# An attention and feed-forward kernel: the first batch's start rearranged, and the halves of the attention weights made on ScalarE and GpSimd

## The chip, the cores and the metric

The kernel runs on one core of one Trainium2 chip. The metric is the device time of one launch in microseconds (us). Each kernel was run several times, and medians and ranges are given.

## The reference

```python
B, N, m, C = 4, 12416, 32, 128                 # x: (B, N, C); inducing: (m, C)

def mab(q, kv):
    s = scale * (q @ kv.transpose(0, 2, 1));  s = s - s.max(-1, keepdims=True)
    a = np.exp(s);  a /= a.sum(-1, keepdims=True) + 1e-09
    return a @ kv

h = mab(I, x)                                  # 32 inducing points look at all tokens
x = mab(x, h).reshape(B * N, C)                # each token looks at the 32 points

rms = np.sqrt(np.mean(x * x, axis=-1, keepdims=True) + 1e-06)
xn = x / rms * rms_g
g = xn @ w_gate                                # 128 -> 1536
silu = g * (1.0 / (1.0 + np.exp(-g)))
return (silu * (xn @ w_val)) @ w_out           # 1536 -> 128
```

The weights arrive as 64-bit numbers and are rounded to 32 bits on the chip.

## The kernel before

The kernel has two parts in time. The **start-up** (to about 61 us) loads x of the first batch, makes its scores and h, and rounds the first weights. The **feed-forward part** follows: some 1,200 steps, each with two products with the gate and value weights (`L600`, `L605`), a silu on ScalarE, a multiplication on VectorE (`u`) and a product with `w_out` (`L550`). The later batches' attention work is threaded through these steps. The parts that matter here:

```python
def warm(n):                                   # products without use, to hold TensorE's clock
    ps = ps_acc.tile([P, 512], F32, name="acc")
    for _ in range(n):
        nc.tensor.matmul(ps[:, 0:P], ident[:], ident[:], start=True, stop=True)
...
def parts():                                   # rounding, step 1 (VectorE): exponent e and fraction f
    ...
    nc.vector.tensor_scalar(out=e[:], in0=high, scalar1=20, scalar2=0x7FF, ...)
    nc.vector.tensor_scalar(out=e[:], in0=e[:], scalar1=896.0, scalar2=1151.0, op0=ALU.max, op1=ALU.min)
    nc.vector.tensor_scalar(out=f[:], in0=high, scalar1=0xFFFFF, scalar2=None, op0=ALU.bitwise_and)
def place(engine): ...                         # step 2 (ScalarE or GpSimd): as floating point
def join(): ...                                # step 3 (VectorE twice, then a product on GpSimd)
```

At a **seam** (one of 27 places, after the first tile, where the next tile of tokens is prepared) the attention weights are turned and cut into a rounded part and a rest, both for TensorE:

```python
def split():
    aT = work.tile([P, 512], F32, name="aT", tag="work")
    nc.vector.transpose(out=aT[rows, 0:w], in_=sc[b][rows, cols2[s]])
    hi, lo = split_of[b, s] = [halves.tile([P, 512], F32R, name=k) for k in ("hi", "lo")]
    nc.vector.tensor_copy(out=hi[rows, 0:w], in_=aT[rows, 0:w])
    nc.vector.tensor_tensor(out=lo[rows, 0:w], in0=aT[rows, 0:w], in1=hi[rows, 0:w].bitcast(F32), op=ALU.subtract)
```

In part of the steps the product with `w_out` is made as three quick ones (a **split product**) instead of one slow one. Its operands cost two operations on ScalarE and two subtractions on GpSimd, some 2.6 us of GpSimd:

```python
nc.scalar.activation(hi, v, AF.Copy, scale=1.0 - 2.0 ** -13)          # v is u
nc.gpsimd.tensor_tensor(out=lo, in0=v, in1=hi.bitcast(F32), op=ALU.subtract)
def rest():
    hs = third.tile([P, 512], F32, name="hs")
    nc.scalar.activation(hs[:, 0:T], hi.bitcast(F32), AF.Copy, scale=2.0 ** -12)
    nc.gpsimd.tensor_tensor(out=d, in0=hs[:, 0:T], in1=lo.bitcast(F32), op=ALU.subtract)
```

A planner decides at build time which steps are split. It keeps an account of when GpSimd is free; `seam_busy` is time of GpSimd that it leaves for a seam's steps (step 5 is `split`):

```python
seam_busy[at] = seam_busy.get(at, 0) + {2: 1.4, 3: 3.0, 4: 1.2}.get(i, 0)
...
free = max(free, now) + busy.get(k, 0) + seam_busy.get((b, u, j), 0)
begin = max(free, now + 2.2 * SLOT)
if (... begin > now + 3.2 * SLOT ...):
    continue                                   # no split product in this step
free = begin + SPLIT
```

## Time and profile before

| | |
|---|---|
| time, first three runs | 1717.77 us median (1717.04 to 1718.19) |
| profiled span, granted clock | 1715.7 us, 0.996 |
| TensorE busy | 1675.3 us (98%) |
| first feed-forward product | at 60.72 us |
| last part | a row of 1,200 steps; a quiet one takes 1.33 us, with a split product 1.17 us |

TensorE is nearly always busy, so the end is set by it alone; what can be won is the time in which it waits or does work of no use. The table of waits of TensorE from 140 to 1690 us names the first kind (what waits, `<-` what released it: us in all, times, longest):

```profile
PE gv L600 <- ACT silu L602: 6.0, 9, 1.0
PE gv L600 <- DVE u L607: 5.9, 9, 0.7
PE acc L550 <- DVE u L607: 4.2, 9, 1.0
```

The second and third lines: some 10 us of waiting for `u`, in pieces of up to 1 us. `u` is made by VectorE, which is only 69% busy, so something stands in front of it now and then.

### The profile page before, as it was taken

The page shows a single profiled execution, that of the slowest core. Times are in us where ns is not written, and L with a number is a line of the kernel's source. Part 1 is how long each engine was busy: PE and PEld are TensorE (multiplying, and loading weights), DVE is VectorE, ACT ScalarE, POOL GpSimd, SP SyncE. Part 2 cuts the span into 40 slices and gives each one's busy share as a digit, 9 for nine tenths or more (in the row PEclk, how much of TensorE's full clock was granted, in tenths as well). Part 3 has the DMA queues.
Part 4 walks back from the last instruction along what each step waited for, and adds up shares of the span by engine and source line. Part 5 has one row for each costly group of instructions (what it writes and reads, how often), then busy time and mean ns, then how long its engine had stood idle before and what let it go on. Part 6 is the DMA issues. An engine that isn't in the chain of part 4 may idle for free. (4 is left out here: it accounts for less than half of the span.)

```text
span 1715.7 us, 23430 instructions
## 1 busy us (share of the span) xinstructions
PE 1675.3 (98%) x6855; PEld 1046.2 (61%) x6855; DVE 1189.4 (69%) x1982; ACT 1222.4 (71%) x2180; POOL 1181.4 (69%) x936
## 2 busy tenths in 40 slices
PE   9899999999999999999999999999999999999998
PEld 7545565655566656665556656566556666666666
DVE  4867876777668776667667877667767666666665
ACT  4346777676777777776777777767677887788786
POOL 0317775776487776676657877577657888888875
PEclk9999999999999999999999999999999999999999
DMA  6344433433343232434334314153211121112111
GB/s 248 87 68 74 81 69 78 103 80 64 62 79 63 47 71 41 105 76 91 67 59 83 58 34 83 36 129 77 50 30 35 32 38 31 35 34 37 31 36 24
DMA packets 389359, 112.65 MB, mean 66 GB/s; under 512 B 365136, under 2 KB 369776, under 8 KB 386672
## 3 DMA queue, kind: packets, MB, share of 16 engines
q1 hardware_dynamic: 388944, 111.02, 32.3%
q8 instruction: 54, 0.88, 0.2%
q14 instruction: 73, 0.60, 0.1%
q10 hardware_dynamic: 288, 0.15, 0.0%
HBM read 53.95 MB, written 27.00 MB: 47 GB/s over the span
## 5 line engine op out<-in xcount | busy, mean ns | idle before, releaser
L607 DVE TENSOR_TENSOR u<-silu,gv 128x512 f32<-128x512 f32 (+2 forms) x1200 | 788.2, 665 | 471.9 <-PE gv L605 276.6
L602 ACT ACTIVATE silu<-gv 128x512 f32<-128x512 f32 (+2 forms) x1200 | 698.6, 584 | 414.7 <-PE gv L600 377.2
L550 PE MATMUL acc<-u,wo 128*128 128x512 f32 (+2 forms) x1598 | 793.9, 581 | 7.0 <-DVE u L607 5.8
L605 PE MATMUL gv<-a,sv 128*128 128x512 f32 (+2 forms) x1200 | 768.1, 640 | 1.3 <-ACT silu L602 0.7
L588 POOL TENSOR_TENSOR xn<-u,xn 128x512 fp32r<-128x512 f32 (+2 forms) x401 | 507.8, 1266 | 314.7 <-ACT xn L587 250.0
L593 POOL TENSOR_TENSOR xn<-hs,xn 128x512 fp32r<-128x512 f32 (+2 forms) x401 | 507.0, 1264 | 53.4 <-POOL xn L588 16.7
L600 PE MATMUL gv<-a,sg 128*128 128x512 f32 (+2 forms) x1200 | 492.5, 410 | 14.3 <-ACT silu L602 6.5
L600 PEld LDWEIGHTS gv<-a,sg 128*128 128x128 f32 x1200 | 227.6, 190 | 255.3 <-ACT silu L602 117.1
L550 PEld LDWEIGHTS acc<-u,wo 128*128 128x128 f32 x1598 | 299.1, 189 | 87.5 <-issue 17.9
L605 PEld LDWEIGHTS gv<-a,sv 128*128 128x128 f32 x1200 | 227.7, 190 | 196.5 <-issue 142.3
L587 ACT ACTIVATE xn<-u 128x512 fp32r<-128x512 f32 (+2 forms) x401 | 248.1, 619 | 18.8 <-DVE u L607 18.1
L592 ACT ACTIVATE hs<-xn 128x512 f32<-128x512 f32 (+2 forms) x401 | 246.3, 614 | 8.8 <-POOL xn L593 8.2
L550 PE MATMUL acc<-xn,xn 128*128 128x512 f32 (+2 forms) x401 | 159.0, 396 | 6.2 <-POOL xn L593 5.9
L568 PE MATMUL u<-xn,xn 128*128 128x512 f32 (+2 forms) x401 | 155.8, 388 | 0.0
L566 PE MATMUL u<-xn,xn 128*128 128x512 f32 (+2 forms) x401 | 155.4, 388 | 0.0
L492 POOL TENSOR_TENSOR rs<-ms,mhalf 128x16 f32<-128x16 f32 (+2 forms) x28 | 75.5, 2698 | 43.0 <-DVE ms L490 42.9
L550 PEld LDWEIGHTS acc<-xn,xn 128*128 128x128 f32 x401 | 75.3, 188 | 29.9 <-POOL xn L593 14.1
L568 PEld LDWEIGHTS u<-xn,xn 128*128 128x128 f32 x401 | 75.4, 188 | 17.1
L566 PEld LDWEIGHTS u<-xn,xn 128*128 128x128 f32 x401 | 75.3, 188 | 15.6
L559 DVE STREAM_TRANSPOSE o<-o 128x512 f32<-128x512 f32 (+2 forms) x97 | 67.7, 698 | 3.4
L558 DVE TENSOR_TENSOR o<-acc,o 128x512 f32<-128x512 f32 (+2 forms) x97 | 64.9, 669 | 0.0
L571 ACT ACTIVATE o<-u 128x512 f32<-128x512 f32 (+2 forms) x97 | 56.4, 582 | 0.2
(155 smaller groups left out, 746.2 us busy)
## 6 DMA issues: line engine op xcount, KB each, us to landing
out_dram<-o SPq DMA_DIRECT2D x320, 64.0 KB, 2.0
xT<-in_x_dram SPq DMA_DIRECT2D x60, 256.0 KB, 4.6
xn<-in_x_dram SPq DMA_DIRECT2D x60, 256.0 KB, 4.4
a<-hi SPq DMA_DIRECT2D x160, 64.0 KB, 2.0
a<-lo SPq DMA_DIRECT2D x158, 64.0 KB, 2.0
w<-w SPq DMA_DIRECT2D x22, 256.0 KB, 3.2
xn<-in_x_dram SPq DMA_DIRECT2D x5, 1024.0 KB, 10.8
out_dram<-o SPq DMA_DIRECT2D x64, 60.0 KB, 2.0
```

Of the source, the lines that this page charges most:

```text
L492: nc.gpsimd.tensor_tensor(out=rs, in0=ms, in1=mhalf[rows, 0:n], op=ALU.pow)
L550: nc.tensor.matmul(acc[:, 0:T], lhsT, rhs, start=st["left"] == NJ, stop=st["left"] == 1)
L566: nc.tensor.matmul(ups[:, 0:T], w[:, i, :], hi, start=st["k"] == nk, stop=False)
L568: nc.tensor.matmul(ups[:, 0:T], w[:, NK + i, :], lo, start=False, stop=not st["k"])
L587: nc.scalar.activation(hi, v, AF.Copy, scale=1.0 - 2.0 ** -13)
L588: nc.gpsimd.tensor_tensor(out=lo, in0=v, in1=hi.bitcast(F32), op=ALU.subtract)
L592: nc.scalar.activation(hs[:, 0:T], hi.bitcast(F32), AF.Copy, scale=2.0 ** -12)
L593: nc.gpsimd.tensor_tensor(out=d, in0=hs[:, 0:T], in1=lo.bitcast(F32), op=ALU.subtract)
L600: nc.tensor.matmul(g[:, 0:T], sg[:, ts(j, P)], a[:, 0:T], start=True, stop=True)
L602: nc.scalar.activation(sl[:, 0:T], g[:, 0:T], AF.Silu)
L605: nc.tensor.matmul(v[:, 0:T], sv[:, ts(j, P)], a[:, 0:T], start=True, stop=True)
L607: nc.vector.tensor_tensor(out=t[:, 0:T], in0=sl[:, 0:T], in1=v[:, 0:T], op=ALU.mult)
```

## The change

It wants three things: (a) a quicker start, with fewer warm-up products, raw weights read only behind all of x, h.T straight out of the summing product (one transpose and some small steps less), and weights rounded beside TensorE's sums; (b) late weights placed on ScalarE in place of GpSimd, which lets their four clamping steps on VectorE go (three more go for weights that ScalarE placed already, so two of nine stay); (c) at the seams, the halves off VectorE: `hi` on ScalarE, `lo` on GpSimd, with 1.4 us of GpSimd kept free for it in the planner. One more edit rides along: the second subtraction of a split product reads `u` instead of `lo`, with another scale, for the same value.

```diff
-    warm(24)
+    warm(10)
...
         def put():
-            if unread:
+            puts.append((i, c))
+            for _ in range((1, 3, 2, 1, 0, 0, 0, 0, 0)[len(puts) - 1]):
                 fetch_raw(*unread.pop(0))
...
-            nc.vector.tensor_scalar(out=e[:], in0=e[:], scalar1=896.0, scalar2=1151.0, op0=ALU.max, op1=ALU.min)
+            if clamp:
+                nc.vector.tensor_scalar(out=e[:], in0=e[:], scalar1=896.0, scalar2=1151.0, op0=ALU.max, op1=ALU.min)
...
-                    if engine is nc.scalar:
+                    if engine is nc.scalar and t is st["e"]:
+                        nc.scalar.activation(to[:], t[:], AF.Relu, bias=bias[:], scale=mul)
+                    elif engine is nc.scalar:
...
-        def end_h():
-            ... fold product, + 1e-9, reciprocal of 128x1, h = product * rec
         def turn_h():
-            ps = st["ps"] = bank()
-            nc.tensor.transpose(ps[:, 0:P], st["h"][:], ident[:])
+            ps, hl = bank(), st["hl"]
+            f = fold[:].rearrange("p q m -> p (q m)")
+            nc.tensor.matmul(ps[:, P:2 * P], hl[:, C:C + 1].to_broadcast((P, P)), f, start=True, stop=True)
+            nc.tensor.matmul(ps[:, 0:P], hl[:, 0:C], f, start=True, stop=True)
+            rec = once.tile([P, P], F32, name="rec")
+            nc.vector.reciprocal(out=rec[:], in_=ps[:, P:2 * P])
             hT = st["hT"] = once.tile([P, P], F32, name="hT")
-            nc.vector.tensor_copy(out=hT[:], in_=ps[:, 0:P])
+            nc.vector.tensor_tensor(out=hT[:], in0=ps[:, 0:P], in1=rec[:], op=ALU.mult)
...
-            nc.vector.tensor_copy(out=hi[rows, 0:w], in_=aT[rows, 0:w])
-            nc.vector.tensor_tensor(out=lo[rows, 0:w], in0=aT[rows, 0:w], in1=hi[rows, 0:w].bitcast(F32), op=ALU.subtract)
+            if b or s:
+                nc.scalar.copy(out=hi[rows, 0:w], in_=aT[rows, 0:w])
+            else:
+                nc.vector.tensor_copy(out=hi[rows, 0:w], in_=aT[rows, 0:w])
+            engine.tensor_tensor(out=lo[rows, 0:w], in0=aT[rows, 0:w], in1=hi[rows, 0:w].bitcast(F32), op=ALU.subtract)
...
-                nc.scalar.activation(hs[:, 0:T], hi.bitcast(F32), AF.Copy, scale=2.0 ** -12)
-                nc.gpsimd.tensor_tensor(out=d, in0=hs[:, 0:T], in1=lo.bitcast(F32), op=ALU.subtract)
+                nc.scalar.activation(hs[:, 0:T], hi.bitcast(F32), AF.Copy, scale=1.0 + 2.0 ** -12)
+                nc.gpsimd.tensor_tensor(out=d, in0=hs[:, 0:T], in1=v, op=ALU.subtract)
...
-    f["end_h"]()
-    warm(6)
-    f["turn_h"]()
     join(2, 0)
     place(0, 1)
+    f["sum_end"]()
+    warm(4)
+    f["turn_h"]()
+    warm(4)
...
-    warm(22)
+    f["stack_of"](0, 0)
+    warm(8)
...
-                (0, place, 0, 2, nc.gpsimd), ...
-                (1, parts, 1, 2), (2, place, 1, 2, nc.gpsimd), (2, join, 0, 2),
+                ... (1, join, 0, 2),
+                (1, parts, 1, 2), (2, place, 1, 2), (3, join, 1, 2),
...
-                seam_busy[at] = seam_busy.get(at, 0) + {2: 1.4, 3: 3.0, 4: 1.2}.get(i, 0)
+                seam_busy[at] = seam_busy.get(at, 0) + {2: 1.4, 3: 3.0, 4: 1.2, 5: 1.4}.get(i, 0)
```

More of the change, by code (lines that the diff above doesn't have):

```diff
@@ L161 @@
     make_identity(nc, ident[:])
+    bias = const.tile([P, 1], F32, name="bias")
+    nc.vector.memset(bias[:], -896.0 * (1 << 23))
     ones = const.tile([P, 1], F32, name="ones")
@@ L188 @@
     chunks = [(i, c) for c in range(NC) for i in ((0, 1, 2) if not c else (0, 1))] + [(2, c) for c in range(1, NC)]
-    places, raw = [], {}
+    places, raw, puts = [], {}, []
     wide = moe_w_gate.dtype != F32
@@ L216, in put, with parts @@
                 nc.sync.dma_start(out=w32[i][c][:], in_=st["dst"])
-            if unread:
+            puts.append((i, c))
+            for _ in range((1, 3, 2, 1, 0, 0, 0, 0, 0)[len(puts) - 1]):
                 fetch_raw(*unread.pop(0))
-        def parts():
+        def parts(clamp=False):
             if i < 2:
@@ L271, in open_ @@
             st["gmx"] = small.tile([P, NS], F32, name="gmx")
+            gram[b] = small.tile([P, P], F32, name="gram")
+            nc.gpsimd.memset(gram[b][:], 0.0)
         def bank():
@@ L344, in turn_e @@
         def turn_e(s):
-            e = st["e", s] = work.tile([P, per[s] * m], F32, name="e", tag="work")
-            nc.vector.transpose(out=e[:], in_=sc[b][:, cols1[s]])
+            e = st["e", s] = (work.tile([P, per[s] * m], F32, name="e", tag="work") if b else
+                              up.tile([P, 512], F32, name="u"))[:, 0:per[s] * m]
+            nc.vector.transpose(out=e, in_=sc[b][:, cols1[s]])
         def sum_h(s):
@@ L361, in sum_h, with sum_end @@
                 nc.vector.tensor_tensor(out=hl[rows, 0:C], in0=hl[rows, 0:C], in1=ps[rows, 0:C], op=ALU.add)
-            elif end:
+            elif end and b:
                 nc.vector.tensor_copy(out=hl[:, 0:C], in_=ps[:, 0:C])
-        def end_h():
-            ps = bank()
-            nc.tensor.matmul(ps[:, 0:C + 1], fold[:].rearrange("p q m -> p (q m)"), st["hl"][:], start=True, stop=True)
-            rec = small.tile([P, 1], F32, name="rec")
-            nc.vector.tensor_scalar_add(out=rec[:], in0=ps[:, C:C + 1], scalar1=1e-9)
-            nc.vector.reciprocal(out=rec[:], in_=rec[:])
-            h = st["h"] = once.tile([P, C], F32, name="h")
-            nc.vector.tensor_scalar_mul(out=h[:], in0=ps[:, 0:C], scalar1=rec[:])
-        def turn_h():
-            ps = st["ps"] = bank()
-            nc.tensor.transpose(ps[:, 0:P], st["h"][:], ident[:])
+        def sum_end():
+            nc.vector.tensor_copy(out=st["hl"][:, 0:C], in_=st["ps"][:, 0:C])
+        def turn_h():
+            ps, hl = bank(), st["hl"]
[4 more added lines that the diff above has]
+            nc.vector.reciprocal(out=rec[:], in_=ps[:, P:2 * P])
             hT = st["hT"] = once.tile([P, P], F32, name="hT")
-            nc.vector.tensor_copy(out=hT[:], in_=ps[:, 0:P])
+            nc.vector.tensor_tensor(out=hT[:], in0=ps[:, 0:P], in1=rec[:], op=ALU.mult)
             if b:
@@ L383, in scale_h @@
             hg = st["hg"] = once.tile([P, P], F32, name="hg")
-            nc.vector.tensor_scalar_mul(out=hg[:], in0=st["ps"][:, 0:P], scalar1=gam[:])
+            nc.vector.tensor_scalar_mul(out=hg[:], in0=st["hT"][:], scalar1=gam[:])
         def square_h():
@@ L389, in square_h @@
                 scale_h()
-            gram[b] = small.tile([P, P], F32, name="gram")
-            nc.gpsimd.memset(gram[b][:], 0.0)
             stacks[b] = [stk.tile([P, F], F32R, name=n) for n in ("sg", "sv")]
@@ L615, with parts @@
     f = attention(0, B > 1)
-    reads = chunks[:len(places)]
-    unread = chunks[len(places):]
+    unread = list(chunks)
     for s in range(NS):
         load_rows(0, s)
-        if reads and s in (0, 2):
-            fetch_raw(*reads.pop(0))
-    for one in reads:
-        fetch_raw(*one)
+        if s in (0, 2):
+            fetch_raw(*unread.pop(0))
     weight = {one: rounding(*one) for one in chunks}
-    def parts(i, c):
-        weight[i, c][0]()
+    def parts(i, c, clamp=False):
+        weight[i, c][0](clamp)
     def place(i, c, engine=nc.scalar):
@@ L635 @@
     f["open_"]()
-    early = [(step, i) for i in range(2) for step in (parts, join)]
+    early = [lambda i=i, first=first: (parts(i, 0, True), place(i, 0, nc.vector)) if first else join(i, 0)
+             for i in range(2) for first in (True, False)]
     for s in range(NS):
@@ L642 @@
         if s and early:
-            step, i = early.pop(0)
-            step(i, 0)
-            if step == parts:
-                place(i, 0, nc.vector)
+            early.pop(0)()
     f["scores1"](NS - 1)
@@ L662 @@
     parts(0, 1)
-    warm(4)
-    f["end_h"]()
-    warm(6)
-    f["turn_h"]()
     join(2, 0)
     place(0, 1)
+    f["sum_end"]()
+    warm(4)
+    f["turn_h"]()
+    warm(4)
     ps = f["scores"](0, f["st"]["hT"][:, 0:m], R, per2[0])
     f["square_h"]()
-    warm(22)
+    f["stack_of"](0, 0)
+    warm(8)
     f["scores2"](0, ps)
@@ L680 @@
     join(0, 1)
-    for i in range(2):
-        f["stack_of"](i, 0)
+    f["stack_of"](1, 0)
     warm(16)
@@ L685 @@
     scale()
+    for i in range(2):
+        f["stack_low"](i, 0)
     parts(1, 1)
     place(1, 1)
-    for i in range(2):
-        f["stack_low"](i, 0)
     apply()
@@ L697 @@
     parts(0, 2)
+    place(0, 2)
     flowing.append(True)
@@ L715, in schedule @@
             for k, step, *args in (
-                (0, place, 0, 2, nc.gpsimd), (0, f["stack_of"], 1, 1), (0, f["stack_low"], 1, 1),
-                (1, parts, 1, 2), (2, place, 1, 2, nc.gpsimd), (2, join, 0, 2),
-                (3, parts, 2, 1), (4, join, 1, 2), (4, place, 2, 1, nc.gpsimd), (5, f["stack_of"], 0, 2), (5, f["stack_low"], 0, 2),
+                (0, f["stack_of"], 1, 1), (0, f["stack_low"], 1, 1), (1, join, 0, 2),
+                (1, parts, 1, 2), (2, place, 1, 2), (3, join, 1, 2),
+                (3, parts, 2, 1), (4, place, 2, 1), (5, f["stack_of"], 0, 2), (5, f["stack_low"], 0, 2),
                 (6, f["stack_of"], 1, 2), (6, f["stack_low"], 1, 2), (6, join, 2, 1),
-                (7, parts, 2, 2), (8, place, 2, 2, nc.gpsimd), (10, join, 2, 2),
+                (7, parts, 2, 2), (8, place, 2, 2), (10, join, 2, 2),
             ):
@@ L743, in schedule @@
                 add(203 + 7 * s, g["sub_max"], s)
-            for k, name in ((126, "max1"), (128, "max2"), (130, "max3"), (134, "exp1"), (189, "end_h"), (191, "turn_h"),
+            for k, name in ((126, "max1"), (128, "max2"), (130, "max3"), (134, "exp1"), (191, "turn_h"),
                             (193, "square_h")):
```

## The prediction

> **What bounds the kernel now.** I read the page first: busy times, then the chain that ended last.
>
> ```profile
> PE 1675.3 (98%) x6855; PEld 1046.2 (61%) x6855; DVE 1189.4 (69%) x1982; ACT 1222.4 (71%) x2180; POOL 1181.4 (69%) x936
> PE 22%; issue 0%; DVE 0%; ACT 0%; POOL 0%; DVEq 0%; POOLq 0%
> ```
>
> TensorE (PE) is busy 98% and the traced end of the chain is all TensorE. But busy is not useful: warm-up matmuls (L178) and matmuls at a lower clock count too. So I read the start and the seams as timelines, where the diff acts. First, TensorE's timeline of the first 63 us (start, duration, then the wait before it):
>
> ```profile
> 1.36 7.99 PE L178 MATMUL acc<-ident 128*128 128x128 f32 x48 [1.36 <-POOL mhalf L165]
> 9.45 3.71 PE L292 MATMUL gv<-ident,xn 128*128 128x128 f32 x32
> 20.26 1.94 PE L292 MATMUL gv<-ident,xn 128*128 128x128 f32 x16 [0.31 <-DMA xn<-in_x_dram]
> 33.05 6.02 PE L358 MATMUL gv<-xn,e 128*32 128x128 f32 x194
> 43.45 5.16 PE L178 MATMUL acc<-ident 128*128 128x128 f32 x44
> 48.44 1.02 PE L478 MATMUL mm<-eT,gram 128*128 128x512 f32 x2
> 60.72 0.47 PE L600 MATMUL gv<-a,sg 128*128 128x512 f32 x1 [1.53 <-DMA a<-lo]
> ```
>
> The feed-forward part begins at 60.72 us; everything ahead of it is start-up. Two groups of warm-up matmuls stand in the way of real work: the first until 9.35, though the first tile of x landed about 5.0 us after its issue at 0.73 (tile view of x, shortest landing), and the 44 until 48.4, though eT was done at 47.09 (46.38 + 0.71).
>
> Second, the complete timeline where the feed-forward part begins:
>
> ```profile
> 62.17 1.37 DVE L237 TENSOR_SCALAR we<-we 128x512 int32<-128x512 int32 x1
> 63.30 1.12 PE L444 MATMUL mm<-silu,hg 128*128 128x512 f32 x2 [1.88 <-POOL silu L256]
> 71.24 2.08 PE L444 MATMUL mm<-w,hg 128*128 128x512 f32 x2 [2.27 <-POOL w L256]
> 86.79 1.12 PE L550 MATMUL acc<-u,wo 128*128 128x512 f32 x2 [1.01 <-POOL wo L256]
> ```
>
> TensorE waits for weights that VectorE and GpSimd are still rounding. The table by windows gives granted clocks of 0.72 and 0.66 for 65-70 and 70-75 us.
>
> Third, a seam, where the next tile's attention weights are cut in halves:
>
> ```profile
> 197.89 1.67 DVE L503 TENSOR_TENSOR lo<-aT,hi 128x512 fp32r<-128x512 f32 x1
> ...
> 200.21 0.50 PE L600 MATMUL gv<-a,sg 128*128 128x512 f32 x1 [0.71 <-DVE u L607]
> ```
>
> The subtraction (L503) holds VectorE 1.67 us, u comes late, TensorE waits.
>
> **What the Trainium skill says.** (1) "SBUF — State Buffer", Who interferes with whom: VectorE and GpSimd share a port pair as an exclusive lock; a VectorE instruction with two SBUF inputs contends with a GpSimd one that reads SBUF, and so does a one-input VectorE instruction in a 2-port mode. The trace agrees: L503 takes 0.69 us when GpSimd is idle and 1.61 us in the median; L237 takes 0.43, but 1.37 beside a GpSimd product. (2) "TensorE: Matmul & The Clock Gate", What's actually happening: the array is at half clock until about 3.4 us of sustained work and falls back after an idle window. The trace agrees roughly: 7 matmul records per us from 3 to 6 us, 11 to 12 at 7 to 9. (3) "VectorE: DVE Perf Modes", First, the fixed hardware budget: the reciprocal is an iterative divide with a repeat count of 8. The trace has it only on 128x1 (0.16 us). My estimate for the new 128x128 form from that page, if the repeats cost a cycle each: 128 x 8 / 0.96 GHz = 1.07, plus 0.16, so 1.2 us. (4) The clock-gate page, Architectural detail, says that ScalarE and VectorE are strict FIFO: rounding put on ScalarE stands in front of the next silu.
>
> **The change part by part.**
>
> *Loading x.* 14 fewer warm-ups, and three raw weights (0.5 MB each) no longer in the queue just behind x. TensorE can start at about 5.8 instead of 9.45, gaining 3.6 if it alone decided. But DMA is at 300 to 460 GB/s until 28 us: six x tiles and two raw weights are 7.3 MB, at 410 GB/s 17.7 us from 2.8, so the sixth tile lands at 20.5 to 21.5 (the first rounded weight is then written and the third raw one read). In before it landed near 22.9 (issued 5.8, 17.1 to landing) and 4.2 us of work followed its transposes' start at 23.12 (to 27.33). The new end is about 25.4: **-1.9**. A cold clock on the first transposes would cost TensorE 1.6, hidden under this limit.
>
> *Summing h.* The exponentials get more buffers (up to eight instead of three). TensorE's 97 summing products take 5.94 us from 33.05 and are almost continuous: **-0.3**. Two parts and a join (some 2.2 us of VectorE) go into this stretch, where VectorE is free from its last transpose until the sums end (2.7 us).
>
> *h.T by the product.* Before, from the fold's end at 40.38 to hT at 42.15 is 1.77 us through four small VectorE steps, one TensorE transpose and the crossings. After: reciprocal 1.2 (estimate) and a multiplication 0.3 plus crossings, 1.6: **-0.2**. hg no longer follows a join: **-0.2**.
>
> *Warm-ups.* 22 become 8 plus one weight product of 0.86 us, ending some 2.6 us earlier; TensorE is then free when eT comes. Of 1.35 us (48.44 - 47.09) I take **-1.1**; VectorE has a join in between.
>
> *Start of the feed-forward part.* In 60-80 us the matmuls counted (20 of L600/L605, 14 records of L550/L444) are worth 20 x 0.2335 + 14 x 0.4315 = 10.7 us at full clock: 9.3 lost. Four clamps go (0.43 to 1.37 each) and GpSimd's placing, and the join for 71.24 comes three steps earlier. Against it, ScalarE takes 8 placings of 0.62 us in front of silus, each waiting for VectorE, and the first gap (1.88) stays because its chain stays. Following the order of the two compiled programs, VectorE reaches u6 about as late as before; I take **-1.5** of 9.3, a choice.
>
> *Seams.* Step lengths (L600 to L600) exceed the quiet ones, 1.33 us plain and 1.17 with a split product, by 16.6 us summed over the 26 later seams; about 14 of it belongs to the halves (the rest beside an exponential). With hi on ScalarE (0.6) and lo on GpSimd (1.28), VectorE keeps only the 0.7 us transpose: I take **-11.4**, some 80%.
>
> *Fewer split products.* The planner now reserves 1.4 us of GpSimd per seam, and the compiled programs have 383 split products instead of 401: 18 x (1.33 - 1.17) = **+2.9**.
>
> *Later batches.* The long reciprocal sits on VectorE three times: **+0.5**. Changing the subtraction's second operand to u keeps its length: 0.
>
> Sum: -1.9 - 0.3 - 0.4 - 1.1 - 1.5 - 11.4 + 2.9 + 0.5 = -13.2. 1717.8 - 13.2 = 1704.6, so **1705 us**.
>
> **Rivals.** *ScalarE becomes the wait.* The silu wait for TensorE (377 us in all, in short pieces) says that it has room; but one stuck placing or hi copy stops silu. If that gave back the start's gain and half the seams', 1712. *GpSimd becomes the wait.* At 69% and 1.28 us per operation it now gets 27 subtractions; split products already wait for L593 3.2 us after 140 us. If seams gain only 5, 1711. *The start gains fully.* If DMA stops limiting and the weights' gaps vanish with the cold clock, the start gives 12 instead of 5: 1698. *The loading is hidden anyway:* if weights read later arrive late for parts, their wait replaces the first saving: 1707.
>
> **Range and chances.** Start -1 to -11 and steady part -2 to -12, seldom both at an extreme: 1697 to 1712. Two per cent is 34 us, more than all lost time that the diff touches (some 9 in the start's ramp, 14 at seams, 5 ahead). Faster 0.02, within 2% 0.97, slower 0.01.
>
> **What would show it.** First transposes near 5.8 and the sixth x tile near 21; score end near 25.4; first L600-type product near 57; reciprocal near 1.2 us; no 2.27 us wait at the third late weight; no VectorE halves beyond the first; TensorE's waits for u at seams gone; 383 split products. Wrong if silus wait for placings, if late raw weights stall VectorE, or if TensorE waits for GpSimd at seams.

## The result, and the profile after

| | before | after |
|---|---|---|
| median (range) of 4 runs each | 1717.51 us (1717.04 to 1718.19) | 1709.34 us (1707.92 to 1710.3) |
| ratio, 95% interval | 1 | 0.9951 (0.9934 to 0.9969) |
| profiled span | 1715.7 us | 1708.1 us |
| split products | 401 | 383 |

The change gains 8 us, within 2%.

The page of the kernel after, busy times and the chain that ended last:

```profile
PE 1668.0 (98%) x6781; PEld 1036.0 (61%) x6781; DVE 1145.0 (67%) x1914; ACT 1224.3 (72%) x2179; POOL 1146.2 (67%) x919
PE 87%; ACT 4%; DVE 3%; issue 2%; POOL 2%; DMA 1%; SPq 1%; ACTq 0%; DVEq 0%; POOLq 0%
```

VectorE has 44 us less to do, but the end has moved by 8: that is the first sign that its work was mostly not on the path. To see where the 8 us arose I took the start of each feed-forward step (its first product with the gate weights) in both traces and subtracted. The **lag** after minus before, in us:

```
step        0     2     8    14    84    96   300   600   900  1188
lag     -0.96 +0.05 +1.06 +1.33 +1.74 +0.97 +0.25 -1.76 -3.73 -7.60
```

So the start-up gained 1.0 us, the first 14 steps lost 2.3, and from there on 8.9 us were gained. The prediction's total (-13.2) misses by 5; its split (start -3.7, first steps -1.5, the rest -8.0) misses most in the first two.

TensorE's timeline of the start-up, after:

```profile
5.79 1.97 PE L301 MATMUL gv<-ident,xn 128*128 128x128 f32 x16 [0.36 <-DMA xn<-in_x_dram]
10.63 3.18 PE L301 MATMUL gv<-ident,xn 128*128 128x128 f32 x16 [2.88 <-DMA xn<-in_x_dram]
...
26.94 1.12 PE L310 MATMUL gv<-xT,indT 128*32 128x480 f32 x16
...
33.72 5.65 PE L368 MATMUL gv<-xn,u 128*32 128x128 f32 x194
...
47.04 1.12 PE L485 MATMUL mm<-eT,gram 128*128 128x512 f32 x2 [0.63 <-DVE eT L479]
...
59.76 0.47 PE L610 MATMUL gv<-a,sg 128*128 128x512 f32 x1 [2.73 <-DMA a<-lo]
```

TensorE does begin on x at 5.79 instead of 9.45, but then it waits 2.88 us for the second tile, which it begins at 10.63 and transposes in 3.18 us, where a tile takes 1.97 at full clock: the granted clock was 0.66 from 10 to 15 us (1.00 before). The scores end at 28.06 (26.94 + 1.12); before, they ended at 27.39. The first feed-forward product waits 2.73 us for its operand (1.53 before): TensorE is through with its work ahead of that wait 2.2 us earlier (57.02 against 59.18, the ends of the last warm-up products), and 1.2 of it is waited away.

All engines' timeline of the first feed-forward steps, after:

```profile
65.75 0.60 ACT L612 ACTIVATE silu<-gv 128x512 f32<-128x512 f32 x1 [0.20 <-PE gv L610]
...
67.96 1.49 DVE L243 TENSOR_SCALAR o<-sc 128x512 int32<-128x512 int32 x1
...
69.37 0.68 DVE L617 TENSOR_TENSOR u<-silu,gv 128x512 f32<-128x512 f32 x1
69.48 0.63 ACT L252 ACTIVATE o<-o 128x512 f32<-128x512 int32 x1 [0.68 <-DVE o L243]
70.02 1.06 ACT L612 ACTIVATE silu<-gv 128x512 f32<-128x512 f32 x2
70.10 0.79 PE L615 MATMUL gv<-a,sv 128*128 128x512 f32 x1 [2.96 <-DVE u L617]
```

The join for the third late weight came earlier and its wait of 2.27 us is gone. In its place TensorE waits 2.96 us, for the `u` at 69.37. Its silu was done at 66.35 (65.75 + 0.60); what held it were VectorE's own steps in front of it, the join (from 66.42 on) and the next weight's first steps, of which the masking (L243) took 1.49 us next to GpSimd's join product. ScalarE had to wait for the same masking with a placing (L252), and the next silu (70.02) stood behind that. And the clock was granted at 0.50 from 70 to 75 us (0.66 before).

TensorE's waits from 140 to 1690 us, after:

```profile
PE gv L610 <- ACT silu L612: 8.3, 15, 1.0
PE acc L560 <- POOL xn L603: 3.4, 6, 0.7
PE acc L560 <- DVE u L617: 1.5, 6, 0.3
```

The seam's wait for `u` in front of the gate product (5.9 us) is gone, as planned. The wait for silu grew from 6.0 in 9 places to 8.3 in 15.

### The profile page after: what moved, and what is told of

Same layout as the page of the kernel before. It is cut to its first block, busy times and chain, and to the rows that moved or that the text cites. A ratio compares the mean times of both kernels' runs of the same rounds, so it can differ in the third digit from the quotient of the medians.

```text
span 1708.1 us, 23142 instructions
## 1 busy us (share of the span) xinstructions
PE 1668.0 (98%) x6781; PEld 1036.0 (61%) x6781; DVE 1145.0 (67%) x1914; ACT 1224.3 (72%) x2179; POOL 1146.2 (67%) x919
## 4 chain that ended last, share of the span: by engine, by line
PE 87%; ACT 4%; DVE 3%; issue 2%; POOL 2%; DMA 1%; SPq 1%; ACTq 0%; DVEq 0%; POOLq 0%
PE acc L560 40%; PE gv L610 16%; PE gv L615 14%; PE u L578 5%; PE u L576 5%; PE mm L310 2%; DVE u L617 1%; PE mm L485 1%; ACT silu L612 1%; PE mm L368 1%; DVE aT L507 1%; PE gv L301 1%; ACT hi L510 1%; ACT hs L602 1%; POOL xn L603 1%
## 5 line engine op out<-in xcount | busy, mean ns | idle before, releaser
L560 PE MATMUL acc<-u,wo 128*128 128x512 f32 (+2 forms) x1634 | 811.5, 581 | 4.4 <-DVE u L617 3.1
L598 POOL TENSOR_TENSOR xn<-u,xn 128x512 fp32r<-128x512 f32 (+2 forms) x383 | 482.2, 1259 | 356.0 <-ACT xn L597 295.1
L603 POOL TENSOR_TENSOR xn<-hs,u 128x512 fp32r<-128x512 f32 (+2 forms) x383 | 481.9, 1258 | 23.2 <-ACT hs L602 22.0
L560 PEld LDWEIGHTS acc<-u,wo 128*128 128x128 f32 x1634 | 305.1, 189 | 84.6 <-issue 18.2
L597 ACT ACTIVATE xn<-u 128x512 fp32r<-128x512 f32 (+2 forms) x383 | 237.0, 619 | 15.6 <-DVE u L617 13.9
L602 ACT ACTIVATE hs<-xn 128x512 f32<-128x512 f32 (+2 forms) x383 | 235.7, 615 | 4.5 <-POOL xn L603 3.1
L560 PE MATMUL acc<-xn,xn 128*128 128x512 f32 (+2 forms) x383 | 149.7, 391 | 6.1 <-POOL xn L603 6.1
L578 PE MATMUL u<-xn,xn 128*128 128x512 f32 (+2 forms) x383 | 149.2, 390 | 0.0
L576 PE MATMUL u<-xn,xn 128*128 128x512 f32 (+2 forms) x383 | 147.8, 386 | 0.0
L578 PEld LDWEIGHTS u<-xn,xn 128*128 128x128 f32 x383 | 71.9, 188 | 15.6
L576 PEld LDWEIGHTS u<-xn,xn 128*128 128x128 f32 x383 | 72.1, 188 | 14.0
```

Source lines behind the costliest of these rows:

```text
L560: nc.tensor.matmul(acc[:, 0:T], lhsT, rhs, start=st["left"] == NJ, stop=st["left"] == 1)
L576: nc.tensor.matmul(ups[:, 0:T], w[:, i, :], hi, start=st["k"] == nk, stop=False)
L578: nc.tensor.matmul(ups[:, 0:T], w[:, NK + i, :], lo, start=False, stop=not st["k"])
L603: nc.gpsimd.tensor_tensor(out=d, in0=hs[:, 0:T], in1=v, op=ALU.subtract)
```

## The experiments

Twelve kernels ran, on one chip at a time with the kernel before beside them. I compare lags between step 48 (after the start and the first seam) and step 1188, the **steady part**, as well as times. Two executions of the same start-up differ by about 1 us in step 0's lag, so a single start is not to be trusted to better than that. Between steps 14 and 48 most kernels shift by less than 0.25 us; before_reserve, halves_back and composed_lo_gpsimd gain 1.5 to 1.6 there, which the steady part leaves out.

| kernel | time, us (range) | ratio (95%) | lag at step 48 | at 1188 | steady part |
|---|---|---|---|---|---|
| after | 1709.34 (1707.92–1710.3) | 0.9951 (0.9934–0.9969) | +1.50 | -7.60 | -9.1 |
| halves_back | 1704.05 (1702.72–1704.54) | 0.9916 (0.9901–0.9931) | +0.04 | -15.18 | -15.2 |
| no_reserve | 1707.42 (1706.65–1708.0) | 0.9935 | +1.66 | -9.45 | -11.1 |
| hi_scalar | 1710.46 (1710.28–1710.98) | 0.9955 | +1.70 | -6.93 | -8.6 |
| lo_gpsimd | 1702.64 (1702.23–1703.35) | 0.991 (0.9895–0.9925) | +0.78 | -14.55 | -15.3 |
| before_reserve | 1708.29 (1708.15–1709.11) | 0.9943 (0.9928–0.9958) | +0.19 | -9.69 | -9.9 |
| before_operand | 1715.63 (1714.85–1716.4) | 0.9986 (0.9974–0.9999) | +1.38 | -1.88 | -3.3 |
| before_res_operand | 1705.78 (1705.07–1707.74) | 0.9932 (0.9919–0.9946) | +0.34 | -11.73 | -12.1 |
| operand_old | 1705.2 (1704.78–1706.33) | 0.9927 (0.9915–0.994) | +0.77 | -12.68 | -13.4 |
| warm_24 | 1709.06 (1708.01–1710.81) | 0.9948 | +1.67 | -7.47 | -9.1 |
| placings_gpsimd | 1708.73 (1707.5–1711.09) | 0.9946 | -0.48 | -8.79 | -8.3 |
| composed | 1702.35 (1701.55–1702.72) | 0.9907 (0.9892–0.9922) | -0.14 | -15.54 | -15.4 |
| composed_lo_gpsimd | 1700.73 (1699.47–1703.81) | 0.9903 (0.9889–0.9916) | -1.45 | -17.14 | -15.7 |

### Does moving the halves pay at all? (halves_back, no_reserve)

My theory was the prediction's: VectorE's halves make `u` late, moving them away pays, and the planner's reserve is a price for it. The rival: the reserve alone removes the collision, and where the halves are made matters little. halves_back takes them home and keeps the reserve; no_reserve keeps them moved and drops it.

```diff
-            if b or s:
-                nc.scalar.copy(out=hi[rows, 0:w], in_=aT[rows, 0:w])
-            else:
-                nc.vector.tensor_copy(out=hi[rows, 0:w], in_=aT[rows, 0:w])
-            engine.tensor_tensor(out=lo...)
+            nc.vector.tensor_copy(out=hi[rows, 0:w], in_=aT[rows, 0:w])
+            nc.vector.tensor_tensor(out=lo...)
```

> The changed kernel with both halves of the attention weights made on VectorE again, the planner's 1.4 us reserve (and so 383 split products) kept. Theory A, port lock: lo was slow on VectorE only because GpSimd held the shared port; with the reserve GpSimd is idle there, lo takes 0.7 us in the median, not 1.61, and most of the seams' gain stays: 1710 to 1712 us. Theory B, VectorE's load at the seam as such: lo stays near 1.6 us, the steps of 2.0 us come back, and the gain of about 9 plus the lost split products is gone: 1718 to 1721 us.

```diff
-                ... {2: 1.4, 3: 3.0, 4: 1.2, 5: 1.4}.get(i, 0)
+                ... {2: 1.4, 3: 3.0, 4: 1.2}.get(i, 0)
```

> The changed kernel without the planner's reserve of 1.4 us: 401 split products again, halves on ScalarE and GpSimd. If GpSimd has room, 18 steps become 0.16 us shorter: -2.9, about 1706.5 us. Rival, the reserve is needed: lo pushes a split product's second subtraction back, TensorE waits up to 1.3 us for it at some of the 26 seams, and the time is 1709 to 1716 us.

halves_back is 5.3 us **faster** than the kernel after, faster than either theory had it. Mine has fallen: moving the halves cost time. no_reserve is about 2 us faster than after too, in the steady part by 2.0 (-11.1 against -9.1), where I had put +2.9 on the reserve. So with the halves moved the reserve costs, and yet with the halves at home it must gain. The next runs take the two apart.

### The reserve alone, in the kernel before (before_reserve)

```diff
-                ... {2: 1.4, 3: 3.0, 4: 1.2}.get(i, 0)
+                ... {2: 1.4, 3: 3.0, 4: 1.2, 5: 1.4}.get(i, 0)
```

> The kernel BEFORE with one token added: the planner's 1.4 us reserve at the last step of each seam; all else as before, both halves on VectorE. If the gain at the seams comes from the reserve alone (GpSimd idle, so lo takes 0.69 us and not 1.61), nearly all of the 16.6 us that the seams' steps exceed the quiet ones goes, less 2.9 for 18 split products: 1703 to 1705 us. Rival: the other subtraction operand (u in place of lo) or something else of the change is needed too: 1709 us or more.

This one number makes 1708.29 us out of 1717.5: as much as the whole change, although it gives up 18 split products. It falls between what the theory (1703 to 1705) and the rival (1709 or more) had asked; the next sections say what was missing. One seam out of the timelines of all engines, before:

```profile
1434.68 1.48 POOL L588 TENSOR_TENSOR xn<-u,xn 128x512 fp32r<-128x512 f32 x1
...
1435.04 1.67 DVE L503 TENSOR_TENSOR lo<-aT,hi 128x512 fp32r<-128x512 f32 x1
...
1436.63 1.27 DVE L607 TENSOR_TENSOR u<-silu,gv 128x512 f32<-128x512 f32 x2
1437.36 0.50 PE L600 MATMUL gv<-a,sg 128*128 128x512 f32 x1 [0.70 <-DVE u L607]
```

and the same seam in before_reserve:

```profile
1429.09 0.69 DVE L503 TENSOR_TENSOR lo<-aT,hi 128x512 fp32r<-128x512 f32 x1
...
1429.70 1.88 DVE L607 TENSOR_TENSOR u<-silu,gv 128x512 f32<-128x512 f32 x3
...
1430.56 0.40 PE L600 MATMUL gv<-a,sg 128*128 128x512 f32 x1
```

Before, GpSimd starts a subtraction of a split product at 1434.68 and its second one follows. VectorE's `lo`, with two inputs in SBUF, begins at 1435.04 and lasts 1.67 us; `u` can start only at 1436.63, and TensorE waits 0.70 us. With the reserve GpSimd has nothing to do just there: `lo` takes 0.69 us, and TensorE does not wait. This is the exclusive port of the Trainium skill ("SBUF — State Buffer", Who interferes with whom), and the case agrees with it over the whole run: before, all 17 `lo` beside which GpSimd was busy took 1.33 to 1.67 us, and all 11 others 0.41 to 0.70; in before_reserve GpSimd is busy beside none. The tile view of `lo` (duration in ns min/median/max), of before and of before_reserve:

```profile
L503 DVE TENSOR_TENSOR lo<-aT,hi x28: 411/1602/1668, 57.0 to 1682.4; 128x512 fp32r<-128x512 f32 x20, 128x480 fp32r<-128x480 f32 x4, 32x256 fp32r<-32x256 f32 x4
```

```profile
L503 DVE TENSOR_TENSOR lo<-aT,hi x28: 414/691/693, 57.7 to 1673.3; 128x512 fp32r<-128x512 f32 x20, 128x480 fp32r<-128x480 f32 x4, 32x256 fp32r<-32x256 f32 x4
```

Not every seam lost by it: comparing step by step, 12 steps became shorter by 0.59 to 1.11 us, together 10.6 us, and many longer by 0.16 us each where a split product was given up. The seam above is step 984, one of the 12: it took 2.02 us, and then 1.16.

### Which half costs? (hi_scalar, lo_gpsimd)

```diff
             if b or s:
                 nc.scalar.copy(out=hi...)
...
-            engine.tensor_tensor(out=lo...)
+            nc.vector.tensor_tensor(out=lo...)
```

> The changed kernel with lo back on VectorE and hi left on ScalarE, reserve kept. Theory, ScalarE's queue: 1709 to 1710, the silu behind hi late by as much as in the changed kernel, TensorE's waits for silu 8 us after 140 us. Rival, GpSimd's lo costs: 1704 to 1705.

```diff
-            if b or s:
-                nc.scalar.copy(out=hi...)
-            else:
-                nc.vector.tensor_copy(out=hi...)
+            nc.vector.tensor_copy(out=hi...)
             engine.tensor_tensor(out=lo...)
```

> The changed kernel with hi back on VectorE and lo left on GpSimd, reserve kept. Theory, ScalarE's queue: the 5 us between the changed kernel (1709.3) and both halves back (1704.0) come from hi standing on ScalarE, waiting 1.4 us for aT in front of a silu; then this run is at 1704 to 1705. Rival, GpSimd's 1.28 us for lo is what costs: 1708 to 1709.

It is `hi` on ScalarE and nothing else: hi_scalar takes 1710.5 us, lo_gpsimd 1702.6. In the steady part -8.6 against -15.3, and the latter is what halves_back has (-15.2). One seam of the kernel after shows why (all engines):

```profile
1429.01 0.70 DVE L507 STREAM_TRANSPOSE aT<-sc 128x512 f32<-128x512 f32 x1
...
1429.75 0.62 ACT L510 CAST hi<-aT 128x512 fp32r<-128x512 f32 x1 [1.39 <-DVE aT L507]
...
1430.28 1.78 ACT L612 ACTIVATE silu<-gv 128x512 f32<-128x512 f32 x3
...
1430.92 0.19 PEld L610 LDWEIGHTS gv<-a,sg 128*128 128x128 f32 x1 [0.76 <-ACT silu L612]
```

and the same seam in halves_back:

```profile
1422.55 0.60 ACT L609 ACTIVATE silu<-gv 128x512 f32<-128x512 f32 x1 [0.21 <-PE gv L607]
...
1422.99 0.70 DVE L507 STREAM_TRANSPOSE aT<-sc 128x512 f32<-128x512 f32 x1
...
1423.72 0.60 ACT L609 ACTIVATE silu<-gv 128x512 f32<-128x512 f32 x1 [0.57 <-DVE aT L507]
1423.73 0.43 DVE L509 CAST hi<-aT 128x512 fp32r<-128x512 f32 x1
```

The same silu starts 0.44 us ahead of VectorE's transpose in halves_back (1422.55), but 1.27 us behind it in the kernel after, so 1.71 us later, because `hi` stands in front of it, for whose `aT` ScalarE had waited 1.39 us. TensorE's next gate product, due 1.32 us after its forerunner, came after 1.61. The same delay repeats: hi_scalar against lo_gpsimd has 17 steps that are longer by 0.22 to 0.65 us, 6.2 us together, at the seams; three of them are followed by a step that is 0.28 shorter. ScalarE is 72% busy and 0.6 us more at a seam is little; what costs is that it takes its instructions strictly in order, and one that waits for VectorE makes the next silu wait too.

### The second subtraction's operand (operand_old, before_operand, before_res_operand)

halves_back has both halves where before_reserve has them, and yet its steady part is 5.3 us better (-15.2 against -9.9). The suspect was the operand, to which the prediction had given nothing.

```diff
-                nc.scalar.activation(hs[:, 0:T], hi.bitcast(F32), AF.Copy, scale=2.0 ** -12)
-                nc.gpsimd.tensor_tensor(out=d, in0=hs[:, 0:T], in1=lo.bitcast(F32), op=ALU.subtract)
+                nc.scalar.activation(hs[:, 0:T], hi.bitcast(F32), AF.Copy, scale=1.0 + 2.0 ** -12)
+                nc.gpsimd.tensor_tensor(out=d, in0=hs[:, 0:T], in1=v, op=ALU.subtract)
```

This is before_operand against before; before_res_operand has the reserve's edit as well; operand_old is halves_back with this edit reversed.

> The kernel before with nothing changed but the operand of that subtraction (u instead of lo, and the scale that belongs to it). The order of instructions is the same on all engines. Operand theory: about 5 us less, 1713 us, and GpSimd's waits of the second subtraction for the first (16.7 us in 30 waits in the trace of before) gone. Rival: 1717.5 us, since those waits are hidden; the VectorE subtraction at the seams stays at 1.6 us.

> The kernel before with the planner's reserve (1708.3 us alone) and the operand. If both gains add: about 1702 to 1704 us, like lo_gpsimd and composed, without any of the moves of the change. If the operand does nothing: 1708. If the reserve has made it void (GpSimd has slack then): between, 1706.

> The kernel after with both halves on VectorE (as in halves_back, 1704.05 us), and with the second subtraction of a split product reading lo again instead of u. Operand theory: halves_back beat before_reserve by 4.2 us although its start was slower, because with u as operand GpSimd's second subtraction need not wait for its first; then taking the operand back costs about 5 us, 1709 us in all, spread thinly over the steps and not at the seams. Rival: the gain is from other parts of the change (buffers, h.T by the product), and this kernel takes 1704 like halves_back.

The operand is worth something, but only half of what I had expected: -3.3 us in the steady part without the reserve, -2.2 with it (-12.1 against -9.9), -1.8 the third time (-15.2 against -13.4); in times, by the ratios, about 2 us each time. In before_operand the order of all instructions on all engines is that of before, so this is the operand alone. With the reserve the gain does not lie in every step: 5 steps, between 289 and 907, are shorter by 0.14 to 0.31 us, and a stretch behind 300, 600 and 900 is shorter by some 0.45. These are the ends of the batches, where the tiles are narrower (480 and 256 columns instead of 512). The timeline of all engines near step 889, before_reserve and then before_res_operand:

```profile
1311.01 1.21 POOL L593 TENSOR_TENSOR xn<-hs,xn 128x480 fp32r<-128x480 f32 x1
...
1311.44 1.05 DVE L502 CAST hi<-aT 128x512 fp32r<-128x512 f32 x1
```

```profile
1309.40 1.23 POOL L593 TENSOR_TENSOR xn<-hs,u 128x480 fp32r<-128x480 f32 x1
...
1310.21 0.71 DVE L502 CAST hi<-aT 128x512 fp32r<-128x512 f32 x1
```

The GpSimd subtraction ends 0.99 us ahead of step 889's gate product in the first (1312.22 to 1313.21) and 1.37 us in the second (1310.63 to 1312.00), so it overlaps less with VectorE's copy, which is 0.34 us shorter. The waits of GpSimd's second subtraction for its first (13.1 us in before_reserve) are gone, but mostly turned into waits for ScalarE's `hs` (21.6 us), which is why the gain is small.

**What stays open.** Between before_res_operand (-12.1) and halves_back (-15.2) 3.1 us remain. Steps of 0.13 us and more explain +0.6 in the wrong direction (the long reciprocal, below). So some 3.7 us are spread over all steps at about 0.003 us each, without one wait to name. operand_old against before_reserve shows the same 3.5. In no_reserve against before, too, the steps that differ by less than 0.1 us add up to 4.0. I did not find the cause: it belongs to the rest of the change (other buffers, thus other places in memory, and fewer instructions), and no run separates these.

### The start: warm-up products and placings (warm_24, placings_gpsimd)

```diff
-    warm(10)
+    warm(24)
```

> The changed kernel with the first 24 warm-ups instead of 10. Theory, cooled clock: with 10, TensorE starts on x at 5.8 but then waits 2.9 us for the second tile of x and does that tile at a lower clock (3.18 instead of 1.97 us); with 24 it starts at 9.45, never waits for that tile, and the scores end at 27.4 as in the kernel before instead of 28.1: -0.7 us over all. Rival, DMA decides the end of the scores whatever TensorE does: no change within 0.2 us of the scores' end.

```diff
-                ... (1, parts, 1, 2), (2, place, 1, 2), (3, join, 1, 2), ...
+                (0, place, 0, 2, nc.gpsimd), ...
+                (1, parts, 1, 2, True), (2, place, 1, 2, nc.gpsimd), (3, join, 1, 2), ...
```

> The changed kernel with the four late placings (and their clamps) on GpSimd, as in the kernel before. Theory, ScalarE's queue: placings stand in front of silus, and TensorE's wait of 2.96 us for u at 70.1 and the loss of 2.3 us against the kernel before from the first feed-forward step to the fifteenth come from that; the wait shrinks below 1 us and the time falls by about 2 us to 1707. Rival, the clock: the 2.73 us gap ahead of the first feed-forward product leaves TensorE cold and the same loss stays: 1709 us, within 0.5.

warm_24 is equal to the kernel after, 1709.06 against 1709.34 us. TensorE starts on x at 9.85 and has one wait left in the loading (TensorE's timeline of warm_24):

```profile
21.26 1.94 PE L301 MATMUL gv<-ident,xn 128*128 128x128 f32 x16 [0.92 <-DMA xn<-in_x_dram]
```

It does the second tile at full clock and ends the scores at 28.39 instead of 28.06. So the theory of the cooled clock, which asked for 27.4 and 0.7 us, has fallen, and the 14 warm-up products less are hidden behind the loading. Nor did x land earlier without weights in between: the fifth tile was waited for at 20.26 before, and at 21.26 here.

How the second tile goes after that wait differs from trace to trace, and I found no cause. In eight traces with the early start its 16 transposes took 1.94 to 3.49 us; for example, in TensorE's timeline of placings_gpsimd, whose start-up code is that of the kernel after:

```profile
10.90 1.94 PE L301 MATMUL gv<-ident,xn 128*128 128x128 f32 x16 [2.93 <-DMA xn<-in_x_dram]
...
69.55 0.50 PE L615 MATMUL gv<-a,sv 128*128 128x512 f32 x1 [1.63 <-DVE u L617]
```

There the tile took 1.94 us and the scores ended at 27.18. Since a single trace misleads here, I averaged over those kernels that share code up to step 14. Four kernels with the start of before have at step 0 a mean lag of +0.33 us (0 to +0.70), at step 14 of +0.82 (0 to +1.70). Six with the start of after (after, halves_back, no_reserve, hi_scalar, lo_gpsimd, operand_old) have -0.97 (-1.55 to -0.57) and +1.30 (+0.71 to +1.68). So the new start-up gains 1.3 us, and the new first steps lose 1.8. The balance of +0.5 at step 14 is not shown: the two ranges there overlap.

The placings are part of that loss. From step 0 to 14 the six kernels with placings on ScalarE lose 2.25 to 2.30 us, placings_gpsimd 1.31, and the two compositions below, which also have a longer last warm-up, 0.87 and 0.78 (the four with the first steps of before: 0 to 1.0). The wait for `u` (second line above) is 1.63 us in place of 2.96, not below 1 as expected. VectorE held that `u` no shorter (3.4 us from the end of its silu, 3.0 in the kernel after), but TensorE had come two products further. So a gain of about 1 us lies in the placings and the clamps, which this run moves together; it is too small to show in the times (1708.73 against 1709.34, where 1707 was expected).

### Put together (composed, composed_lo_gpsimd)

composed is the kernel after with both halves on VectorE, the late placings and clamps on GpSimd, `warm(24)` at the beginning and `warm(28)` instead of `warm(16)` in front of the feed-forward part. composed_lo_gpsimd has `lo` on GpSimd, placings and clamps likewise, `warm(28)`, and the short first `warm(10)`.

```diff
-    warm(16)
+    warm(28)
     join(1, 1)
```

> What the first four runs point to, put together on the changed kernel: both halves on VectorE with the reserve; late placings and clamps on GpSimd; 24 first warm-ups; and 12 more warm-ups (28 for 16) to bridge the 2.7 us gap ahead of the first feed-forward product, so that TensorE is not at a lower clock in the first steps. If the clock is what costs the ramp its remaining 1.3 us: 1701 us, and the granted clock in 60-75 us above 0.9. If the ramp waits for rounded weights whatever the clock: 1703 us.

> Composition for the best time: the kernel after with hi on VectorE and lo on GpSimd (1702.6 us alone), the late placings and clamps back on GpSimd, and a longer last group of warm-up products to hold the clock. If the parts add, the ramp gives 1 to 2 us: 1701 us. If the two GpSimd loads collide, 1703 or more.

Both beat before and after: 1702.35 and 1700.73 us. The longer warm-up closed the gap that it was for (composed waits 0.06 us ahead of the first product, in place of 2.73), but the clock did not hold: 0.77 granted from 60 to 75 us (0.69 in the kernel after), where the theory had asked for more than 0.9, and TensorE still waited 1.89 us for a weight and 2.03 for a `u`. Their ratios (0.9907 and 0.9903) can't be told apart, and both are hardly better than lo_gpsimd alone (0.991). The step from 1709.3 to 1702.6 is `hi`; the rest is at the size of the scatter. From the kernel before, two small edits alone (before_res_operand) gave 1705.8.

## Why the prediction was right or wrong

The total was inside the range (1697 to 1712) and the class was right, yet 4.3 us lay between 1705 and 1709.3, and several terms were off by more than that and made up for each other.

- **Loading x (-1.9).** Wrong, for two reasons. The larger is the landing: the sixth tile was to land at 20.5 to 21.5, with x moving at 410 GB/s. It landed at 22.7 (22.9 before); from 2.80 us to then the transfers ran at 372 GB/s. Its line of the view of transfers (last number: us from issue to landing), before and after:

```profile
xn<-in_x_dram SPq DMA_DIRECT2D x1, 960.0 KB, 17.1
```

```profile
xn<-in_x_dram SPq DMA_DIRECT2D x1, 960.0 KB, 17.0
```

  Reading the weights later did not move it by itself: with 24 warm-up products it landed at 23.8 (warm_24, composed). The smaller is the clock: "A cold clock on the first transposes would cost TensorE 1.6, hidden under this limit". It was not hidden: after its slow second tile TensorE waits for no further tile, and the scores end at 28.06, against 25.4 predicted and 27.39 before. Where that tile took 1.94 us (placings_gpsimd, lo_gpsimd, operand_old) they ended at 27.2 to 27.5, so the clock accounts for 0.6 to 0.9 us of the miss of 2.7 in the kernel after, and the rest was missed at full clock too. The rival "the loading is hidden anyway" was right that nothing is won here (the scores end at 27.2 to 28.5 in the eight traces with the early start, at 27.4 to 28.1 in the four with the start of before).
- **Summing h (-0.3).** Right: 5.65 us against 6.02.
- **h.T by the product (-0.4).** The reciprocal took 0.96 us, estimated 1.2. From the end of the sums to hT it is 2.86 us (39.37 to 42.23), before 3.08 (39.07 to 42.15): the -0.2 of this part is right. The -0.2 put on hg was not measured by itself.
- **Warm-ups (-1.1).** Gained as far as the first product with the scores (47.04 against 48.44), but this term failed to ask what waits next: the wait for the transfer of `lo` grew from 1.53 to 2.73 us. The sum of all terms ahead of step 0 is -3.7 predicted, -1.3 in the mean of the traces.
- **Start of the feed-forward part (-1.5).** The wrong sign: +1.8. The prediction named the cost ("8 placings of 0.62 us in front of silus, each waiting for VectorE") and then chose the gain; the wait of 2.27 us went, and one of 2.96 came, with the clock at 0.50 behind it. What ended that wait was VectorE's own queue, a `u` behind a join and a masking step, and not a placing, though moving the placings and clamps back wins about 1 us of the 1.8.
- **Seams (-11.4).** The observation was right, `lo` makes `u` late, and the wait went away. The attribution was wrong: it was not the halves' being on VectorE but GpSimd's split product beside them. The reserve alone gains 9.9 in the kernel before. With the reserve in place moving the halves costs 6.1 (-9.1 against -15.2), all of it through `hi` on ScalarE. Moving them without the reserve would, as an estimate, have gained 5.8: no_reserve gains 11.1, less 5.3 for the operand and the spread rest, which is what halves_back has beyond before_reserve.
- **Fewer split products (+2.9).** As the price of the reserve with the halves moved it measured +2.0 (no_reserve against after). As the effect of the reserve it had the wrong sign, since the term counted what the reserve takes away and not the collision that it prevents. This is the step that failed most: the two views that I quoted, 0.69 us "when GpSimd is idle" and 1.61 in the median (1.60 in the view of `lo` above), said already that an idle GpSimd was enough.
- **Later batches (+0.5).** Right in size: the reciprocal lengthens three steps by 0.35 each (191, 491, 791), and the two VectorE steps that went give back 0.14 each two steps earlier; 0.6 together.
- **The operand (0).** Wrong: -2 to -3.
- **The rivals.** "ScalarE becomes the wait" was the true one at the seams, and said how: a stuck `hi` stops silu. (For the placings this is not shown.) Its 1712 lies 2.7 us above the result, 1705 lay 4.3 below. It was named and given too little weight. "GpSimd becomes the wait" fell: lo_gpsimd costs nothing (1702.6), and the split products' wait for GpSimd stays at 3.4 us (3.2 before).
- **A reading.** The 7 and 11 to 12 matmul records per us count those that only overlap a microsecond; by their starts they are 5 per us from 3 to 6 and 9 from 7 to 9. The conclusion stays.

So the end came out within 5 us partly by luck. Start and first steps were to give 5.2 us and gave nothing clear of the scatter (+0.5 in the mean of the traces). The steady part was to give 8.0 and gave 9.1, but out of other terms: -9.9 by the reserve, +6.1 by `hi` on ScalarE, -2.2 by the operand and -3.1 by what stays open.

## What to carry to other kernels

When an operation takes longer than its quiet duration, first look at what runs beside it: keeping the neighbour away for that moment can be worth more than moving the operation, and costs one number in a planner. Before moving work to an engine with room, ask what it will wait for there and what stands behind it in the same queue; an engine that is 72% busy is no place for an instruction that waits for another engine in front of the critical one. And a change with several parts should be tried part by part: here one number in the planner alone was worth 9 us, and one line cost 6 us.

## What the Trainium skill lacked or had wrong

- "VectorE: DVE Perf Modes", First, the fixed hardware budget: it states that the reciprocal is an iterative divide, without a duration. Here a 128x128 one out of PSUM took 0.96 us; my estimate from the repeat count was 1.2.
- "SBUF — State Buffer", Who interferes with whom: right (0.69 against 1.60 us in the median of the same subtraction). That either side can be the one that pays is on the page too, and seen here: GpSimd's 128x512 subtractions took 1.44 to 1.48 us where they began during `hi` (13 of them) and 1.58 to 1.61 where they began during `lo` (8), against 1.29 in quiet surroundings. Nothing is lacking.
- "TensorE: Matmul & The Clock Gate", What's actually happening: that the window runs free would fit what was seen, but no run here shows the window. It calls the price of the ramp small for a whole kernel; for comparing starts it isn't. The same 16 transposes took 1.94 to 3.49 us in traces with the same loading code, which moves a start by more than the 1.3 us that the change gains there.
- The same page, Architectural detail, on the strict order of ScalarE and VectorE: right, and here with a price, 6.2 us over 17 steps for one waiting 0.6 us copy per seam. No page warns of it as a cost of moving work to an engine with free time.
